# Expert rows of a top-1 mixture: indirect gathers with TensorE transposes replaced by 256-byte reads with a VectorE block transpose

## The chip, the cores and the metric

The kernel runs on one core of a Trainium2 chip. The metric is the device time in microseconds. Engines are named as in the profile: PE is TensorE (PEld its weight loads), DVE is VectorE, ACT is ScalarE, POOL is GpSimd and SP is SyncE, which here only issues DMAs. A name such as L345 is a line of the kernel.

## The reference

A linear attention with a normalised output feeds a mixture of eight experts in which each row goes to one expert.

```python
# q, k, v: (8 batches, 8 heads, 576 rows, 64), g_norm: (64,)
kv  = einsum('bhsd,bhse->bhde', k, v)
out = einsum('bhsd,bhde->bhse', q, kv)
out = out / sqrt(mean(out*out, -1) + 1e-6) * g_norm
x   = out.transpose(0, 2, 1, 3).reshape(4608, 512)      # N = 4608 rows, D = 512

logits = x @ w_gate                                     # (4608, 8)
e      = argmax(logits, 1)
gate   = softmax(logits)[n, e[n]]
y[n]   = gate[n] * (relu(x[n] @ w1[e[n]]) @ w2[e[n]])   # w1: (512, 1024), w2: (1024, 512) per expert
```

All inputs and the output are float32. With the inputs drawn here the experts get between 494 and 600 rows each.

## The kernel before

**Attention.** The loop runs over `b` from 0 to 8. In step `b` the PE work of batch `b` (the products of k and v, transposes of q, a product that folds the routing weights in) is interleaved with output tiles of 128 rows of the batches before it. Nine tiles make a pair of batches `j`; pair 3 ends in step `b == 8`. For a tile, `o_mm` does the products, `o_red` the squares (ACT) and their sums (DVE, `ms`), `o_nrm` the inverse root (ACT, `rs`), and `o_x` writes normalised float16 rows into a row buffer `xrow` of three tiles, of which there are four, and logits into `lhat`. The instructions are issued in the order of the program text; each engine works its own queue in order.

**Routing.** `route` takes a chunk of tiles (`chunks` lists them per pair), finds each row's expert and its place among that expert's rows by prefix sums on PE, and POOL scatters the rows (L743) into a DRAM table `x_slots`: 4608 slots of 516 two-byte words for each expert, 512 for the row and four for gate and row number. `route` is a generator, whose next part is run by `job()` twice per tile step.

**Experts.** A group is an expert and some of its slot tiles of 128. Of experts 0, 1 and 2 the first three tiles come first, as groups 0 to 2, with counts known after two thirds of the rows (`early_rows`); their last two tiles are groups 3 to 5; experts 3 to 7 have five tiles each, groups 6 to 10. One further tile for rows that don't fit (the spill tile, `d_` names) is put ahead of group 10, and a loop after the end takes what even that does not hold. With the inputs used here the spill tile is empty and the loop runs no time.

A group's rows come by `fetch`: POOL gathers 128 slots by an index (L291), where slots beyond the count have an index out of bounds and are skipped, so that the buffer, one of three `xl` set to zero at the start, keeps what it held. `xpose` turns a tile by four PE transposes (L325), and DVE evacuates it, times g_norm, into `xsT` (L328). `stage1` does the first product in eight steps of 128 columns (L345) with a Relu on ACT (L353); `stage2` does the second (L361), DVE multiplies by the gate (`y`, L366), and POOL scatters the result (L369). Both products have two PSUM buffers. The transposes of the next group stand between the `stage2` calls of the current one.

**Weights.** `w_step` casts one staged 512 KB piece to float16 on DVE (L220) and has SP load another (L206, L210). There are four staging buffers, and `w_step` is called at fixed places in the tile steps and the groups.

**End.** The last group's scatters are followed by `fin`, a small memset, and the loop, whose count each engine loads from memory. In the built order of POOL the last output scatter stands behind the loop's test.

Of the kernel before, what the change touches and what calls it, by code (L numbers as in the profile page):

```python
# [45 lines left out]
def kernel(  # L46
# [20 lines left out]
    xs_views = dram_disjoint_views(xs.ap(), NT)  # L67
# [9 lines left out]
    for j in range(4):  # L77
# [20 lines left out]
        "w1off": arf[:, None] + 128.0 * np.array([0, 2, 1, 3], np.float32)[None, :],  # L98
# [36 lines left out]
    nc.scalar.dma_start(g2[64:128, :], g_norm.unsqueeze(1))  # L135
    wgt = P_const.tile([128, 8, 8], F32, tag="wgt")
# [17 lines left out]
    chunks = {0: [(0, 9)], 1: [(0, 9)], 2: [(0, 3), (3, 9)], 3: [(0, 3), (3, 6), (6, 9)]}  # L154
    ohbs, n_route = [], 0
    for j in range(4):
# [7 lines left out]
    xl_ring = [  # L164
        P_const.tile([128, SLOT_TILES, ROW], I16, tag=f"xl{n}", name=f"xl{n}") for n in range(3)
    ]
# [13 lines left out]
    def w_load(pool, bufs):  # L180
# [23 lines left out]
        if n < 4:  # L204
            r0 = 128 * (2 * (n % 2) + n // 2)
            nc.sync.dma_start(st, w1[r0 : r0 + 128, :])  # L206
# [8 lines left out]
        w_staged.append((e, dst, st))  # L215

    def w_cast(engine):
        if w_staged:
            e, dst, st = w_staged.pop(0)
            engine.tensor_copy(dst, st)  # L220
            w_done[e] = w_done.get(e, 0) + 1
# [15 lines left out]
    cnt = P_const.tile([128, 8], F32, tag="cnt")  # L237
    srow = P_const.tile([128, 8, SLOT_TILES], F32, tag="srow")
# [4 lines left out]
    def row_index(name, ctr, ne, nk):  # L243
        bad = P_const.tile([128, ne, nk], F32, tag="bad" + name, name="bad" + name)
        nc.vector.tensor_tensor(
            bad, _bc(cv["srank"][:, 0:nk], 1, ne), _bc(ctr[:, 0:ne], 2, nk), op=ALU.is_ge
        )
        idx = P_const.tile([128, ne, nk], I32, tag="idx" + name, name="idx" + name)
        nc.vector.scalar_tensor_tensor(
            out=idx, in0=bad, scalar=BIG, in1=srow[:, 0:ne, 0:nk], op0=ALU.mult, op1=ALU.add  # L250
        )
        badi = P_const.tile([128, ne, nk], I32, tag="badi" + name, name="badi" + name)
        nc.vector.tensor_scalar(badi, bad, BIG, None, op0=ALU.mult)
        return idx, badi
# [3 lines left out]
    def early_rows():  # L258
# [6 lines left out]
        for i in range(EARLY):  # L265
            groups[i].fetch()
        yield

    def final_rows():
        nc.vector.tensor_tensor(cnt, base[n_route], cv["ebase"], op=ALU.subtract)  # L270
        rows["all"] = row_index("a", cnt, 8, SLOT_TILES)

    class Group:
        def __init__(self, n, e, k0, k1):
# [4 lines left out]
            self.xl = xl_ring[n % 3]  # L279
            self.table = "early" if self.small and k0 == 0 else "all"  # L280

# [6 lines left out]
        def fetch(self):  # L288
            idx = rows[self.table][0]
            for k in range(self.K):  # L290
                nc.gpsimd.indirect_dma_start(  # L291
                    out=self.xl[:, k, :], out_offset=None, in_=xs.ap(),
                    in_offset=IndirectOffsetOnAxis(
                        ap=idx[:, self.e, self.k0 + k : self.k0 + k + 1], axis=0
                    ),
                    bounds_check=E * N - 1, oob_is_err=False,
                )

        def slot_ids(self):
# [4 lines left out]
                self.xl[:, 0 : self.K, D + 2 : D + 4].bitcast(I32),  # L304
                badi[:, self.e, self.k0 : self.k0 + self.K].unsqueeze(2), op=ALU.max,
            )

# [6 lines left out]
        def start(self):  # L314
            self.xsT = self.pool().tile(
                [128, 4, self.n], F16, tag="xsT" + self.tag(), bufs=1, name="xsT"
            )

        def tag(self):
            return ""  # L320

        def xpose(self, k):
            ps = PSA.tile([128, 4, 128], F16, tag="KV", bufs=2, name="xps")
            for c in range(4):
                nc.tensor.transpose(  # L325
                    ps[:, c, :], self.xl[:, k, c * 128 : (c + 1) * 128].bitcast(F16), ident16
                )
            nc.vector.tensor_scalar(  # L328
# [49 lines left out]
    class SpillGroup(Group):  # L378
# [4 lines left out]
        def tag(self):  # L383
            return "d"
# [508 lines left out]
```

## Time and profile before

| what | us |
|---|---|
| median of three runs | 326.77 (325.64 to 333.92) |
| profiled execution | 330.94 |
| its span, from the first to the last instruction | 329.2 |
| PE busy | 269.0 (82%) |
| DVE busy | 183.4 (56%) |
| POOL busy | 137.6 (42%) |
| ACT busy | 119.9 (36%) |
| mean granted PE clock | 0.903 of full |

In a group's line, the numbers after the bar are the busy time in us and the mean of one instruction in ns; after the second bar stands how long the engine had been idle before these instructions, and what ended most of that. In the timeline a row has start, duration, engine, line, operation, output and inputs, and in brackets the idle time before it and what released it. A windows row has the stretch, its length, then busy time and count for PE, PEld, DVE, ACT and POOL, the granted PE clock, the share of the DMA engines and GB/s. In the slices a digit is the busy share in tenths.

### The profile page before, as it was taken

Reading aid. Unit: us, or ns where it says so; the run is one execution under the profiler, and the core shown is the slowest. Engines: PE = TensorE matmul, PEld = TensorE weight load, DVE = VectorE, ACT = ScalarE, POOL = GpSimd, SP = SyncE. Lnnn points to the kernel's source line nnn. Section 1 sums busy time; section 2 is a strip of 40 time slices with the busy share of each in tenths; the row PEclk is TensorE's granted clock in tenths of the full one; section 3 lists DMA queues with packets and bytes.
Section 4 is the critical chain, followed back from the end, with each engine's and each line's share of the span. In section 5 each row is a group of like instructions: output and inputs, shape, how many; then the busy total and the mean of one; then the engine's idle time right before and its main releaser. Section 6 shows DMA issues by size and latency. Waiting matters only on the chain.

```text
span 329.2 us, 7247 instructions
## 1 busy us (share of the span) xinstructions
PE 269.0 (82%) x2759; PEld 189.3 (58%) x2759; DVE 183.4 (56%) x433; ACT 119.9 (36%) x316; POOL 137.6 (42%) x147
## 2 busy tenths in 40 slices
PE   0699897689766977564979996989999999997980
PEld 0587776577656866462535563657565665645630
DVE  6205566346745368889184678344657658375040
ACT  1136564436543445322322431326142240602600
POOL 9100001720076004384675462777477656052041
PEclk9999997959995589555999998999999999999996
DMA  6999999997897016799589894667799999983021
GB/s 158 334 368 367 369 368 367 381 282 216 246 323 295 18 67 167 250 323 324 201 260 372 295 322 121 214 214 251 250 339 358 351 397 279 408 284 130 0 99 55
DMA packets 45395, 85.79 MB, mean 261 GB/s; under 512 B 6188, under 2 KB 22829, under 8 KB 45360
## 3 DMA queue, kind: packets, MB, share of 16 engines
q1 hardware_dynamic: 36736, 66.07, 59.9%
q0 software_dynamic: 6976, 18.96, 15.6%
q10 hardware_dynamic: 1648, 0.29, 0.5%
q8 instruction: 22, 0.36, 0.4%
q14 instruction: 13, 0.11, 0.1%
HBM read 71.77 MB, written 15.50 MB: 265 GB/s over the span
## 4 chain that ended last, share of the span: by engine, by line
PE 26%; issue 11%; DMA 9%; POOL 7%; DVE 5%; POOLq 1%; ACT 0%; DVEq 0%; ACTq 0%
PE hp L345 13%; PE yp L361 11%; DMA out_dram<-y,d_id 7%; POOL out_dram L369 4%; POOL xl L291 2%; DMA xl<-x_slots,idxe 2%; PE xps L325 1%; DVE y L366 1%; DMA x_slots<-xrow,posi 1%; POOL x_slots L743 1%; DVE w1e L220 1%; DVE xsT L328 0%; POOLq L888 0%; POOLq L854 0%; DVE w2e L220 0%
## 5 line engine op out<-in xcount | busy, mean ns | idle before, releaser
L353 ACT ACTIVATE hT<-hp 128x320 f16<-128x320 f32 (+3 forms) x136 | 53.6, 426 | 106.5 <-PE hp L345 105.9
L345 PE MATMUL hp<-xsT,w1e 128*128 128x320 f16 (+2 forms) x512 | 76.6, 306 | 7.2 <-DVE xsT L328 6.3
L361 PE MATMUL yp<-w2e,hT 128*128 128x512 f16 x320 | 74.1, 379 | 0.3 <-DVE y L366 0.3
L369 POOL DMA_INDIRECT out_dram<-y,idv x40 | 44.6, 1115 | 60.3 <-DVE y L366 49.3
L345 PEld LDWEIGHTS <-w1e 128*128 128x128 f16 x512 | 51.0, 100 | 32.1 <-issue 11.7
L651 PE MATMUL ops<-kvx,qT 64*128 64x72 f32 (+1 forms) x640 | 48.0, 310 | 10.5 <-DVE lhat L680 9.6
L743 POOL DMA_INDIRECT x_slots<-xrow,posi x36 | 35.7, 991 | 40.5 <-DVE xrow L739 15.5
L651 PEld LDWEIGHTS ops<-kvx,qT 64*128 64x128 f32 (+1 forms) x640 | 42.3, 215 | 15.0 <-issue 9.3
L361 PEld LDWEIGHTS <-hT 128*128 128x128 f16 x328 | 30.8, 98 | 31.6 <-issue 0.4
L366 DVE TENSOR_SCALAR y<-yp,xl 128x512 f32<-128x512 f32 x40 | 30.0, 750 | 33.6 <-PE yp L361 29.9
L664 DVE TENSOR_REDUCE ms<-sq 128x8 f32<-128x512 f32 x36 | 24.6, 685 | 25.1 <-ACT sq L660 25.0
L291 POOL DMA_INDIRECT xl<-x_slots,idxa x31 | 32.4, 1046 | 11.7 <-issue 7.0
L594 PE MATMUL kvps<-mk,mv 128*64 128x64 f32 x640 | 28.7, 258 | 9.4 <-DMA mv<-in_v_dram 9.1
L676 DVE TENSOR_TENSOR xrow<-ops,rs 128x512 f16<-128x512 f32 x36 | 24.7, 686 | 18.0 <-DMA x_slots<-xrow,posi 9.3
L660 ACT ACTIVATE sq<-ops 128x512 f32<-128x512 f32 x36 | 21.5, 598 | 31.9 <-PE ops L651 31.5
L594 PEld LDWEIGHTS kvps<-mk,mv 128*64 128x64 f32 x640 | 26.0, 168 | 11.8 <-issue 10.3
L710 POOL COPY xrow<-tokc 128x3 int32<-128x3 int32 x12 | 3.0, 253 | 64.3 <-DVE xrow L676 64.2
L582 PE MATMUL tps<-ctile,mq 128*128 128x128 f32 x144 | 26.9, 320 | 3.5 <-ACT qT L583 1.9
L220 DVE CAST w2e<-wst 128x1024 f16<-128x1024 f32 x32 | 22.3, 704 | 11.4 <-DMA wst<-in_moe_w_dram 11.4
L583 ACT COPY qT<-tps 128x384 f32<-128x384 f32 x48 | 21.9, 473 | 14.4 <-PE tps L582 14.4
L328 DVE TENSOR_SCALAR xsT<-xps,g 128x512 f16<-128x512 f16 x41 | 19.2, 477 | 12.9 <-PE xps L325 12.7
L220 DVE CAST w1e<-wst 128x1024 f16<-128x1024 f32 x32 | 21.6, 688 | 4.5 <-DMA wst<-in_moe_w_dram 4.5
(99 smaller groups left out, 184.1 us busy)
## 6 DMA issues: line engine op xcount, KB each, us to landing
wst<-in_moe_w_dram SPq DMA_DIRECT2D x64, 512.0 KB, 5.8
mq<-in_q_dram SPq DMA_DIRECT2D x16, 576.0 KB, 7.8
mk<-in_k_dram SPq DMA_DIRECT2D x16, 320.0 KB, 7.5
mv<-in_v_dram SPq DMA_DIRECT2D x16, 320.0 KB, 7.3
mk<-in_k_dram SPq DMA_DIRECT2D x16, 256.0 KB, 7.9
mv<-in_v_dram SPq DMA_DIRECT2D x16, 256.0 KB, 7.1
wsts<-in_moe_w_dram SPq DMA_DIRECT2D x8, 512.0 KB, 5.9
out_dram<-y,idv POOLq DMA_INDIRECT x40, 4.9
```

The costliest lines, as they stand in the source:

```text
L220: engine.tensor_copy(dst, st)
L291: nc.gpsimd.indirect_dma_start(out=self.xl[:, k, :], out_offset=None, in_=xs.ap(), in_offset=IndirectOffsetOnAxis(ap=idx[:, self.e, self.k ...
L345: nc.tensor.matmul(hp, self.w()[0][:, kk, f * 128 : (f + 1) * 128], self.xsT[:, kk, s : s + self.step], start=(kk == 0), stop=(kk == 3),)
L353: nc.scalar.activation(self.hT[:, f, s : s + self.step], hp, ACTF.Relu)
L361: nc.tensor.matmul(yp, self.hT[:, f, k * 128 : (k + 1) * 128], self.w()[1][:, f, :], start=(f == 0), stop=(f == 7),)
L366: nc.vector.tensor_scalar(y, yp, self.xl[:, k, D : D + 2].bitcast(F32), None, op0=ALU.mult)
L369: nc.gpsimd.indirect_dma_start(out=self.views(k), out_offset=IndirectOffsetOnAxis(ap=self.ids[:, k : k + 1], axis=0), in_=y, in_offset=Non ...
L582: nc.tensor.transpose(ps[:, c, :], src[:, 128 * m : 128 * m + 128], cv["ident"])
L594: nc.tensor.matmul(kvps[b][64 * y : 64 * y + 64, 2 * u + a, :], main["v", b, u][:, 2 * y + a, c, :], main["k", b, u][:, 2 * y + a, c, :], ...
L651: nc.tensor.matmul(ps[p0 : p0 + 64 * n, y, o0 : o0 + 72], qT[b][hs, a, blk // 2 : blk // 2 + n, :].rearrange("d c p -> d (c p)"), kvx[b][h ...
L676: nc.vector.tensor_tensor(xr[:, 0:D].bitcast(F16).rearrange("p (a h d) -> p a h d", a=2, h=4), xv, _bc(rs2, 3, 64), op=ALU.mult,)
L743: nc.gpsimd.indirect_dma_start(out=xs_views[9 * j + t0 + t], out_offset=IndirectOffsetOnAxis(ap=posi[:, t : t + 1], axis=0), in_=xrow[j, ( ...
```

## The change

- The gathers go. `fetch` reads a group's rows, which lie together in `x_slots`, with four plain DMAs into 32 partitions each, in pieces of 128 words (256 B), and the gate and row number with a fifth. They are issued from ACT's queue, but for groups 0 and 1, which SP issues in step `b == 8`.
- Slots beyond the count must then hold zeros in DRAM. `pads` has POOL scatter a row of zeros to them once counts are known; the index of a used slot is out of bounds, so it is skipped. Three groups' `pads` follow the early counts, two groups' the final ones, and the others are issued two or three groups ahead.
- The PE transposes and the `xsT` evacuations go. `xpose` is one DVE instruction for the group that transposes 32x32 blocks, issued after the second `y` of the group before. `stage1` reads the blocks in place. For that the rows of w1 go to PE in another order, and g_norm is applied as a scale in the w1 cast (`g4`). The spill tile keeps PE transposes.
- Also: six `xrow` buffers, not four; the folded product uses the other PSUM pair and both its copies are on ACT; small groups' second product uses that pair too; pair 2 is routed as tiles 0 to 5 and 6 to 8; one more pause in `route`; one `w_step` per tile from step 5 on; in step 8 groups' work begins from its second tile; the zeroing of `xl` and `fin` go; the loop's count is loaded earlier, inside group 7.

```diff
-    chunks = {0: [(0, 9)], 1: [(0, 9)], 2: [(0, 3), (3, 9)], 3: [(0, 3), (3, 6), (6, 9)]}
+    chunks = {0: [(0, 9)], 1: [(0, 9)], 2: [(0, 6), (6, 9)], 3: [(0, 3), (3, 6), (6, 9)]}
...
-            r0 = 128 * (2 * (n % 2) + n // 2)
-            nc.sync.dma_start(st, w1[r0 : r0 + 128, :])
+            nc.sync.dma_start(st, w1.rearrange("(p c) f -> c p f", c=4)[n])
...
+            if n < 4:
+                engine.tensor_scalar(dst, st, g4[:, n : n + 1], None, op0=ALU.mult)
+            else:
+                engine.tensor_copy(dst, st)
...
-        for i in range(EARLY):
-            groups[i].fetch()
+        groups[0].pads()
+        yield
+        groups[1].pads()
+        groups[2].pads()
...
         rows["all"] = row_index("a", cnt, 8, SLOT_TILES)
+        for n in range(EARLY, EARLY + 2):
+            groups[n].pads()
...
-        def fetch(self):
-            idx = rows[self.table][0]
+        def pads(self):
+            pad = rows[self.table][0]
             for k in range(self.K):
                 nc.gpsimd.indirect_dma_start(
-                    out=self.xl[:, k, :], out_offset=None, in_=xs.ap(),
-                    in_offset=IndirectOffsetOnAxis(
-                        ap=idx[:, self.e, self.k0 + k : self.k0 + k + 1], axis=0
+                    out=self.pad_views[k],
+                    out_offset=IndirectOffsetOnAxis(
+                        ap=pad[:, self.e, self.k0 + k : self.k0 + k + 1], axis=0
                     ),
+                    in_=zrow, in_offset=None,
                     bounds_check=E * N - 1, oob_is_err=False,
                 )
+        def fetch(self, engine=nc.scalar):
+            r0 = self.e * N + 128 * self.k0
+            src = xs.ap()[r0 : r0 + self.n].rearrange("(g b) w -> b g w", b=32)
+            self.xl = self.pool().tile([128, self.n // 32, 128], I16, tag="xl", bufs=2, name="xl")
+            for i in range(4):
+                c0 = 128 * (2 * (i % 2) + i // 2)
+                engine.dma_start(self.xl[32 * i : 32 * i + 32], src[:, :, c0 : c0 + 128])
+            self.gi = P_fe.tile([128, SLOT_TILES, 4], I16, tag="gi", bufs=3, name="gi")
+            engine.dma_start(
+                self.gi[:, 0 : self.K],
+                xs.ap()[r0 : r0 + self.n, D:ROW].rearrange("(k p) w -> p k w", p=128),
+            )
+        def xpose(self):
+            g = self.n // 32
+            self.xT = self.pool().tile([128, g, 4, 32], I16, tag="xT", bufs=2, name="xT")
+            nc.vector.transpose(self.xT, self.xl.rearrange("p g (a c) -> p g c a", c=4))
...
-                if f == 0 and 1 <= real and EARLY <= real + 2 < len(groups):
-                    groups[real + 2].fetch()
+                if f == 0 and EARLY - 1 <= real < len(groups) - 3:
+                    groups[real + 3].pads()
...
                 cur.stage2(k)
                 if not cur.small:
                     w_step()
-                while todo and len(todo) > max(cur.K - 2 - k, 0):
-                    nxt.xpose(todo.pop(0))
+                if k == 0 and 0 <= real < len(groups) - 2:
+                    groups[real + 2].fetch()
+                if k == min(1, cur.K - 1) and 0 <= real < len(groups) - 1:
+                    groups[real + 1].xpose()
+                if k == 3 and cur.e == E - 2:
+                    spill.xpose()
...
-            nc.vector.tensor_copy(kvx[b][:, 1], folds[b][1])
+            nc.scalar.copy(kvx[b][:, 1], folds[b][1])
...
-                    [128, 3, ROW], I16, tag="xrow", bufs=4, name=f"xrow{j}{t}"
+                    [128, 3, ROW], I16, tag="xrow", bufs=6, name=f"xrow{j}{t}"
...
-                for _ in range((0, 1, 1, 2)[max(b - 5, 0)]):
+                if b >= 5:
                     w_step()
-                if b == B and n >= 3:
+                if b == B and n == 0:
+                    for i in range(2):
+                        groups[i].fetch(nc.sync)
+                if b == B and n >= 1:
                     unit()
                     unit()
...
-    fin = P_const.tile([128, 1], F32, tag="fin")
-    nc.gpsimd.memset(fin, 0.0)
-    manual.close()
...
-    with tc.For_i(0, n_more) as it:
+    with tc.For_i(0, n_more[0]) as it:
```

## The prediction

> **What bounds the kernel now.** I read, in this order, the page's slices, the windows by stage, the chain that ended last, the timeline where the chain breaks, and the groups by form; a fence for each.
>
> ```profile
> PE   0699897689766977564979996989999999997980
> DVE  6205566346745368889184678344657658375040
> PEclk9999997959995589555999998999999999999996
> DMA  6999999997897016799589894667799999983021
> ```
>
> ```profile
> 153.10:191.65 38.55, 35.60 (x205) 18.69 (x205) 21.08 (x51) 11.90 (x25) 22.14 (x23) 0.96 0.84 293
> 191.65:222.07 30.42, 26.15 (x182) 16.87 (x180) 19.00 (x53) 9.20 (x24) 18.49 (x19) 0.94 0.63 206
> 240.68:259.12 18.44, 18.44 (x126) 11.29 (x125) 11.89 (x24) 6.12 (x16) 13.30 (x13) 1.00 0.97 352
> 320.03:329.20 9.17, 0.00 (x1) 0.00 (x0) 0.75 (x1) 0.00 (x0) 1.60 (x3) 0.67 0.18 68
> ```
>
> A slice is 8.23 us. Up to about 66 us the DMA row is full (input loads). From 66 to 153 us nothing is full. From 153 us, where the expert stage starts, PE sets the time: a five-tile expert takes 18.4 us with PE busy throughout, DVE busy 11.9 and DMA at 0.97. The end, 9.2 us, has no matmul.
>
> ```profile
> 234.82 0.22 PE xps L325 x4
> 235.05 1.73 PE yp L361 x8
> ...
> 240.68 8.69 PE hp L345 x64
> ```
>
> ```profile
> 100.33 0.69 DVE L676 TENSOR_TENSOR xrow<-ops,rs 128x512 f16<-128x512 f32 x1 [5.01 <-DMA x_slots<-xrow,posi]
> 101.26 1.98 PE L651 MATMUL ops<-kvx,qT 64*128 64x72 f32 x16 [3.21 <-DVE lhat L680]
> 153.12 2.72 PE L345 MATMUL hp<-xsT,w1e 128*128 128x384 f16 x8 [2.78 <-DVE xsT L328]
> 202.96 5.54 PE L345 MATMUL hp<-xsT,w1e 128*128 128x256 f16 x32 [3.12 <-DVE xsT L328]
> ...
> 301.16 0.98 POOL L369 DMA_INDIRECT out_dram<-y,d_id  x1 [3.81 <-DVE y L366]
> 325.20 0.98 POOL L369 DMA_INDIRECT out_dram<-y,idv  x1 [4.67 <-issue]
> ```
>
> ```profile
> L328 DVE TENSOR_SCALAR xsT<-xps,g 128x512 f16<-128x512 f16 x41 | 19.2, 477 | 12.9 <-PE xps L325 12.7
> L291 POOL DMA_INDIRECT xl<-x_slots,idxa x31 | 32.4, 1046 | 11.7 <-issue 7.0 <-DMA x_slots<-xrow,posi 2.6 <-PE hp L345 2.1
> ```
>
> In the chain, a tile's transposes cost PE 0.22 us, its second matmuls 1.73, a five-tile first stage 8.69. At 100.33 DVE had stood 5.01 us because row buffers (four) still had scatters in flight, and PE then ran at half clock to about 118. At 202.96 PE waited behind the spill tables on DVE. The last output scatter started at 325.20, 4.4 us after its data (DVE done at 320.82), because the built order puts the loop test ahead of it.
>
> [...] 32 matmuls of 256 columns take 5.54 us after the 3.12 us wait and 4.30 elsewhere. [...]
>
> **Part 1, removed from PE.** 40 x 4 transposes: 40 x 0.22 = 8.8 us on PE's path; the empty spill tile keeps its four. With them go 40 xsT evacuations (19.2 us of DVE).
>
> **Part 2, the block transpose on DVE.** One instruction per group, 512 elements per tile. [...] 1.76 us for three tiles, 1.22 for two, 2.82 for five: 22 us in all, so DVE's sum hardly moves. Its place matters. In the built order it stands behind the second y of the current group. For five tiles: yp of tile 1 ends at 3.46 us of the second stage, y at 4.35, a cast at 4.9, the transpose at 7.7, y of tile 2 at 8.4. yp has two PSUM buffers, so tile 4, due at 6.92, waits until 8.4: 1.5 us lost, against 1.1 us of transposes gained. For two tiles it stands after the last y: the next group starts 4.35 + 1.22 = 5.6 us into a 3.46 us stage, 2.1 us late; ahead of a five-tile group, 3.7 late. For three tiles, 0.85 late. Bounds: a quarter of this price [...] to the full price[...].
>
> **Part 3, casts and small edits.** 32 of the expert casts, and four of the spill's, get a per-partition scale; [...] 0.69 us stays (up to twice that, 0.4 us each more, if not: 14 us of DVE, partly hidden under PE). Eight kvx copies move to ACT (0.39 each), which has room. Eight g4 loads and 8 casts earlier by one stage: hidden under the loads.
>
> **Part 4, early gain.** Six row buffers remove the 5.01 us wait. Five tile steps took 22.9 us from 95.58 to 118.45; at the pace of the warm stretch (seven in 23.2 us from 72.4) they take 16.5. Gain 6.4, so the fifth tile of the last two batches starts near 127, not 133.1.
>
> **Part 5, start of the expert stage.** Counts at about 122 us; POOL: three row scatters, then nine zeroing scatters. The scatter of the spill tile at 301.16 writes nothing (the reference's inputs give 494 to 600 rows per expert, below 640) and still took 0.98 us, so skipping is not cheap: 9 x (0.98 + 0.30) = 11.5 us, from 123.3 to 135, landed near 138 (2.6 us is the shortest landing of such scatters). SP, which waits there, issues 4 reads at 0.65 us (a small-piece load on ACT's queue took 0.67), landing near 143; transpose 1.8; first matmul near 144.9, against 153.1: gain 8.2, the 6.4 included. Weight loads queued behind SP wait with them, one or two of them late, covered by the four staging buffers.
>
> **Part 6, first three groups.** Now three attention tiles and two routing rounds stand between these matmuls. From 144.9: f0 and f1 at half clock 2.7 us; PE then stands 2.9 us for the last routing; at 164 the second half of group 0; block-transpose delays 0.85 + 0.85 + 0.5. ACT's read for group 2 waits for the row scatters of the sixth to third last tiles (landed 165.5), and five issues of 0.65 us hold its Relus until 169: PE 1.6 us late. The read for group 3 waits for the last rows and four zeroing scatters (180.5): 2.3 us more. Group 3 starts near 194.2, 49.3 us after the first matmul; before took 38.5. Loss 10.8.
>
> **Part 7, the two-tile groups.** POOL per group: two outputs and five zeroing scatters, 2 x 1.48 + 5 x 1.28 = 9.4 us, for 7.8 us of matmuls. The read on ACT waits for the newest zeroing scatters, though its own landed long ago, and the first Relus of the next group stand behind it: about +2.2 and +0.6. With the transposes (+1.3 behind the spill tables, +2.05, +1.9), 38.4 us against 30.4. Loss 8.
>
> **Part 8, five-tile groups and end.** Three groups at 17.34 + 1.5 = 18.84 against 18.5: +1.0. In the one before the spill tile, y of tile 2 (8.4) is followed on DVE by a cast, y, a cast and the spill's three copies, so PE starts its last tile near 11.5 instead of 6.92 and ends 21.9 us after the group began, against 17.4: +4.5. The 3.1 us wait at 299.6, for the last group's xsT, goes. Together +2.4. The end gains 3.7, because the last scatter no longer stands behind the loop test: 320.03 + 9.2 becomes the last matmul + 5.5 (y 0.75, issue 1.3, landing 3).
>
> Sum: -8.2 + 10.8 + 8 + 2.4 - 3.7 = +9.3, span 329.2 -> 338.5. The profiled execution took 330.94 around that span; its median of runs is 326.77, ratio 0.987. (338.5 + 1.7) x 0.987 = 336.
>
> **Rivals.** (a) *Cheap block transpose at a quarter of my price* (0.8 us for five tiles). Saved: start 1.2, small groups 2.2, two-tile groups 3.6, five-tile groups 6, and about 2.5 of half-clock time: 15.5, so 323 span, 319 us: faster. For: the data are 2-byte, and 2-byte xsT took 477 ns where 512 single elements from PSUM took 750. [...] It decides below about 0.85 us for five tiles. (b) *Half price* (1.4 us), or the front gaining as much again from the freed PSUM ring: 11 less, 326 us: no change. (c) *DMA becomes the bound.* 20,480 pieces of 256 B and 5,120 of 8 B replace 5,120 rows; DMA stands at 0.97 at 352 GB/s and the fullest windows show 1.07 at 368. If a piece costs 40 ns of an engine, a five-tile group needs 15 us for weights and outputs and 7 for rows, 22 against 18.8: about +12 over the stage, 348 us. [...]
>
> **How the numbers follow.** Forecast 0.50, at 336, own range 328 to 344, of which 0.07 lies within 2%; (c) 0.18; (b) 0.14; (a) 0.18. Slower 0.43 + 0.18 = 0.61, same 0.21, faster 0.18; two per cent is what a measurement of this kernel can tell from no change. The range 314 to 351 takes in most of (a) and (c); outputs and waits that stack in small groups set its upper end.
>
> **What would show it.** Right: no xrow wait near 95 us; first expert matmul near 145; transposes of about 1.8, 1.2 and 2.8 us with PE waiting behind them for y; Relus late behind reads on ACT between 165 and 225; the last scatter within 1 us of its y. Wrong: a five-tile transpose near 1 us or five-tile groups of 17.5 us (a, b); casts waiting for wst in most groups and DMA above 1.0 after 230 us (c); zeroing scatters well under 0.98 us, or ACT never waiting.

## The result and the profile after

The changed kernel takes 371.51 us (median of four runs, 368.7 to 377.48), the kernel before 328.54 (four runs, 325.64 to 333.92): ratio 1.1313, 95% interval 1.1134 to 1.1492. The forecast was slower, 336 us with a range of 314 to 351: the direction is right, the size is not. Of the four executions of each kernel the slowest (377.48 and 333.92) counts as slow, and the ratio is taken over the other three. The profiled execution took 368.7 us, its span 366.9; it is the shortest of the four, and the profiled one of before (330.94) lies above its median, so the stages below account for 37.7 us where the medians are 43.0 apart.

A correction first. The texts above say that the experts get 494 to 600 rows and that the spill tile is empty. Counted again from the reference's inputs, the experts get 564, 494, 600, 572, 539, 654, 585 and 600: expert 5 has 14 rows more than its five tiles hold, so the spill tile holds 14 rows, and the scatter at 301.16 in the trace of before wrote 14 rows, not none. That a scatter which writes nothing takes as long, 0.98 us, is shown by others, the changed kernel's zeroing scatters (last section).

The slices of the page, now 9.17 us each:

```profile
PE   0699999986595226996777176619889498987990
DVE  0106686773688436677178030700855617476030
PEclk9999999999579558699899586757999969998996
DMA  5999999999977376888883518190696799996012
```

Up to about 80 us PE is fuller than before. Then come holes that before did not have: at 120 to 140 us PE falls to 2 tenths, and between 200 and 250 us twice to 1 tenth, with the granted clock at 5 tenths. Windows for the same stages as those shown of before (groups 0 to 2, groups 3 to 5, one five-tile group, the end):

```profile
135.64:187.68 52.04, 42.19 (x224) 21.31 (x224) 31.55 (x73) 14.78 (x35) 23.17 (x25) 0.87 0.81 257
187.68:235.35 47.67, 26.72 (x145) 16.19 (x145) 21.00 (x49) 8.89 (x24) 19.90 (x21) 0.77 0.46 120
266.39:287.20 20.81, 17.80 (x105) 10.16 (x104) 12.93 (x21) 6.02 (x16) 8.37 (x8) 1.00 0.80 277
358.22:366.90 8.68, 0.00 (x0) 0.00 (x0) 0.75 (x1) 0.00 (x0) 1.48 (x2) 0.64 0.21 75
```

In the second row PE is busy 26.72 of 47.67 us (before 26.15 of 30.42), and DMA stands at 0.46: on average neither an engine nor DMA is full, so something waits. The timeline of the group after them, the first five-tile one (group 6), shows who waits for whom:

```profile
232.46 2.83 DVE L327 STREAM_TRANSPOSE xT<-xl 128x2560 int16<-128x2560 int16 x1
...
234.85 1.20 POOL L302 DMA_INDIRECT x_slots<-zrow,pada  x1 [0.30 <-issue]
...
235.35 4.43 PE L363 MATMUL hp<-xT,w1e 128*128 128x320 f16 x16 [3.59 <-DVE xT L327]
...
235.96 1.03 SPq L211 DMA_DIRECT2D wst<-in_moe_w_dram  x2
...
237.22 24.36 SPq L207 DMA_DIRECT2D wst<-in_moe_w_dram  x4
237.31 5.86 ACTq L317 DMA_DIRECT2D xl<-x_slots  x4
...
237.75 1.06 POOL L387 DMA_INDIRECT out_dram<-y,idv  x1 [0.30 <-issue]
...
246.90 0.38 ACTq L319 DMA_DIRECT2D gi<-x_slots  x1
247.33 1.43 ACT L371 ACTIVATE hT<-hp 128x320 f16<-128x320 f32 x4 [18.60 <-DMA xl<-x_slots]
248.14 8.24 PE L363 MATMUL hp<-xT,w1e 128*128 128x320 f16 x48 [8.37 <-ACT hT L371]
...
249.78 0.98 POOL L302 DMA_INDIRECT x_slots<-zrow,pada  x1 [10.96 <-DMA gi<-x_slots]
...
257.71 3.38 ACTq L317 DMA_DIRECT2D xl<-x_slots  x4
```

Read it from PE backwards. PE fills its two PSUM buffers from 235.35, stands from 239.78 on, and goes on 8.37 us later, when a Relu has emptied one. ACT works in order and has reads of `x_slots` ahead of that Relu. They wait for zeroing scatters, the last of which POOL issued at 234.85, and start at 237.31. Up to there ACT has waited and PE has not. What PE then waits for is the reads themselves: the four take 5.86 us to issue, where four at 188.21 take 1.84, and `gi` follows only at 246.90: in the trace its issue waits for the semaphore on which the first of the four counted its landing and on which `gi` then counts its own, and that read landed just before, 9.5 us after its own issue. Four weight loads of 512 KB are in flight with them (two at 235.96 and the first two of the row at 237.22; its other two are issued after 259), and from 238 to 248 us the DMA engines are full: 0.51 of their time goes to weight loads and 0.44 to the reads. So the scatters push the reads out of PE's second stage, in which ACT has nothing to do, into the place where the Relus and the weight loads are.

On POOL the next zeroing scatter (249.78) has waited 10.96 us, until those reads had landed, since it writes the table that they read; only when POOL is through with the scatters can the next reads go (257.71). The two queues hold each other up. They do so by the table as a whole: the reads at 237.31 fetch the rows of group 7, and the scatters that they wait for zero slots of group 8, other rows. Whether a table for each expert would untie them was not tried. And PE, after such waits, does 48 matmuls of 320 columns in 8.24 us, where 64 take 8.86 at a granted clock of 1.00 (340.73 to 349.59).

The waits over the whole execution (total us, times, longest):

```profile
ACT hT L371 <- DMA xl<-x_slots: 63.8, 5, 18.6
...
POOL x_slots L302 <- DMA gi<-x_slots: 41.2, 5, 11.0
PE hp L363 <- ACT hT L371: 34.2, 8, 8.4
...
PE hp L363 <- DVE xT L327: 23.3, 7, 14.0
```

Of the 34.2 us that PE stands behind Relus, 2.7 belong to an attention tile (145.94). In the seven other places PE comes to a stand before the first read has started only in group 2 (171.46, reads from 172.63) and group 4 (201.33, reads from 206.48), 6.3 us together. In the other 25 the scatters have landed, and ACT is issuing the reads that they held back. In group 7 it is again `gi` that comes late (268.42), here behind a weight load that SP issued at 261.26, on whose semaphore it waits and which landed just before, 7.1 us after its issue.

The balance by stage is in the first two rows of the table below: the expert stage starts 17.5 us earlier, groups 0 to 5 take 30.7 longer, groups 6 to 10 with the spill tile 24.9 longer, the end 0.5 less; but for rounding the sum is the 37.7 us of more span.

Of the runs below, beside e5 to e16 the kernel before itself took 353 to 361 us. The traces kept there show a longer attention stage (e13, the changed kernel again, has its first expert matmul at 160.6 us, not 135.6), for a reason that they don't show, so that between these and the others only ratios to the kernel before on the same chip, and stages after the first expert matmul, are compared.

### The profile page after: what moved, and what is told of

Read it like the earlier page. It is cut to its first block, busy times and chain, and to the rows that moved or that the text cites. A ratio compares the mean times of both kernels' runs of the same rounds, so it can differ in the third digit from the quotient of the medians.

```text
span 366.9 us, 6972 instructions
## 1 busy us (share of the span) xinstructions
PE 263.1 (72%) x2599; PEld 174.6 (48%) x2599; DVE 181.9 (50%) x398; ACT 119.5 (33%) x324; POOL 128.0 (35%) x144
## 3 DMA queue, kind: packets, MB, share of 16 engines
q10 hardware_dynamic: 24384, 4.79, 8.0%
## 5 line engine op out<-in xcount | busy, mean ns | idle before, releaser
L363 PE MATMUL hp<-xT,w1e 128*128 128x320 f16 (+2 forms) x512 | 90.0, 339 | 58.2 <-ACT hT L371 34.2
L363 PEld LDWEIGHTS <-w1e 128*128 128x128 f16 x512 | 55.2, 109 | 92.0 <-issue 59.9
L384 DVE TENSOR_SCALAR y<-yp,gi 128x512 f32<-128x512 f32 x40 | 29.7, 741 | 85.5 <-PE yp L379 85.5
L302 POOL DMA_INDIRECT x_slots<-zrow,pada x31 | 31.9, 1030 | 58.5 <-DMA gi<-x_slots 41.2
L699 PE MATMUL ops<-kvx,qT 64*128 64x72 f32 (+1 forms) x640 | 42.9, 285 | 11.1 <-DVE lhat L728 10.3
L699 PEld LDWEIGHTS ops<-kvx,qT 64*128 64x128 f32 (+1 forms) x640 | 37.4, 191 | 17.0 <-DVE lhat L728 8.2
L642 PE MATMUL kvps<-mk,mv 128*64 128x64 f32 x640 | 25.8, 242 | 11.9 <-DMA g<-in_g_norm_dram 8.4
L222 DVE TENSOR_SCALAR w1e<-wst,g 128x1024 f16<-128x1024 f32 x32 | 24.5, 775 | 13.9 <-DMA wst<-in_moe_w_dram 13.9
L642 PEld LDWEIGHTS kvps<-mk,mv 128*64 128x64 f32 x640 | 23.2, 154 | 14.4 <-issue 10.7
L327 DVE STREAM_TRANSPOSE xT<-xl 128x2560 int16<-128x2560 int16 (+2 forms) x11 | 23.2, 2109 | 9.0 <-DMA xl<-x_slots 9.0
L708 ACT ACTIVATE sq<-ops 128x512 f32<-128x512 f32 x36 | 21.6, 601 | 13.4 <-PE ops L699 12.5
```

The costliest lines, as they stand in the source:

```text
L302: nc.gpsimd.indirect_dma_start(out=self.pad_views[k], out_offset=IndirectOffsetOnAxis(ap=pad[:, self.e, self.k0 + k : self.k0 + k + 1], axis=0
L363: nc.tensor.matmul(hp.rearrange("p (g b) -> p g b", b=32), self.w()[0][:, kk, f * 128 : (f + 1) * 128], self.xcols(kk, s), start=(kk == 0) ...
L384: nc.vector.tensor_scalar(y, yp, self.gate(k), None, op0=ALU.mult)
L642: nc.tensor.matmul(kvps[b][64 * y : 64 * y + 64, 2 * u + a, :], main["v", b, u][:, 2 * y + a, c, :], main["k", b, u][:, 2 * y + a, c, :], ...
L699: nc.tensor.matmul(ps[p0 : p0 + 64 * n, y, o0 : o0 + 72], qT[b][hs, a, blk // 2 : blk // 2 + n, :].rearrange("d c p -> d (c p)"), kvx[b][h ...
```

## The experiments

The theory (A): the reads on ACT's queue wait for zeroing scatters in front of the Relus, and the scatters on POOL wait for the reads. Rival B: the reads wait for completion semaphores (slots, in the expectations) that SP's weight loads hold. Rival C: the block transposes and their place on DVE are the loss.

Stages in us, from each trace; the last column has the time (a single execution, or the median where the text gives an interval) and that of the kernel before on the same chip:

| kernel | first expert matmul | groups 0 to 5 | groups 6 to 10 | after the last matmul | time, kernel before beside it |
|---|---|---|---|---|---|
| before | 153.1 | 69.0 | 98.0 | 9.2 | 328.5 |
| changed | 135.6 | 99.7 | 122.9 | 8.7 | 371.5, 328.5 |
| e1 reads on SP | 134.0 | 86.3 | 112.0 | 8.7 | 342.8, 325.4 |
| e2 zeroing after the read | 134.0 | 90.0 | 126.0 | 8.5 | 360.2, 325.4 |
| e3 zeroed once, ACT | 149.8 | 84.1 | 107.2 | 14.8 | 357.8, 325.4 |
| e4 zeroed once, SP | 155.0 | 83.4 | 104.8 | 14.8 | 359.8, 325.4 |
| e5 SP, units later | 163.2 | 86.6 | 110.2 | 9.1 | 370.8, 358.1 |
| e6 and transposes early | 166.2 | 83.5 | 111.9 | 8.8 | 372.2, 358.1 |
| e7 and early tiles by writes | 162.1 | 83.7 | 113.1 | 18.4 | 379.0, 358.1 |
| e8 changed, four xrow | 161.4 | 101.7 | 115.7 | 9.0 | 389.6, 358.1 |
| e9 = e6 | 163.1 | 81.7 | 112.4 | 8.5 | 367.4, 360.6 |
| e10 zeroed on POOL, SP, later, early | 171.9 | 68.5 | 103.2 | 8.4 | 353.8, 360.6 |
| e11 e10, transposes late | 172.7 | 75.6 | 105.6 | 8.4 | 364.1, 360.6 |
| e12 e10, units early | 170.4 | 76.1 | 103.2 | 8.4 | 359.9, 360.6 |
| e13 changed again | 160.6 | 98.6 | 120.6 | 8.2 | 388.7, 353.4 |
| e14 changed, four xrow | 157.9 | 99.0 | 119.5 | 8.9 | 388.8, 353.4 |
| e15 before, front edits | 156.2 | 68.9 | 100.0 | 10.0 | 340.7, 353.4 |
| e17 = e1 | 139.0 | 87.5 | 110.9 | 8.9 | 346.2, 326.8 |
| e18 before, fold ring | 147.5 | 68.1 | 98.5 | 10.5 | 326.9, 326.8 |

**The queue of the reads (e1, e17).**

```diff
-        def fetch(self, engine=nc.scalar):
+        def fetch(self, engine=nc.sync):
```

> All slot reads are issued by SP instead of ACT; the zeroing scatters stay where they are. In the changed kernel PE stood 34.2 us behind Relus (8 times), and the Relus behind reads that waited on ACT. Theory A (the reads on ACT wait for zeroing scatters, and these for earlier reads, in front of the Relus): PE's wait for Relus falls below 8 us, POOL's zeroing scatters still wait for reads (over 20 us of the 41.2), SP's weight loads now stand behind the waiting reads; span 366.9 -> 335 to 345. Rival B (completion slots that the reads share with SP's weight loads are what ACT waits for): the same place is freed, and in SP's own order a slot wait costs nothing new; span near 330 to 340, so A and B are not told apart here. Rival C (the block transposes and their place on DVE cost the time): PE's waits move from Relus to xT, span stays above 358.

> The kernel of e1 (changed kernel with all slot reads on SP's queue), timed. Theory (reads in front of the Relus on ACT are the largest part of the loss): ratio to the kernel before 1.03 to 1.07, where the changed kernel has 1.10 to 1.13. Rival (e1 was a lucky look): ratio 1.09 to 1.13.

Span 341.0 in e1; e17 timed gives ratio 1.0606, interval 1.0528 to 1.0684, against 1.1313. Waits in e1:

```profile
POOL x_slots L302 <- DMA gi<-x_slots: 28.2, 6, 6.0
PE hp L363 <- DVE xT L327: 26.9, 6, 13.6
...
DVE w1e L222 <- DMA wst<-in_moe_w_dram: 21.8, 7, 7.0
...
PE hp L363 <- ACT hT L371: 3.6, 2, 2.7
```

PE's wait behind Relus is 3.6 us instead of 34.2. The scatters still wait for the reads, 28.2 us, and the weight loads, now behind the reads on SP, come late (21.8), but PE has no wait for a cast of them that the trace lists. One word takes back 13.4 us in groups 0 to 5 and 10.9 in groups 6 to 10: 24.3 of the 55.6 that the expert stage had lost. PE's wait for the block transposes stays (26.9, was 23.3), so what came back is not C's; how much C costs is measured with e11 below. A and B aren't told apart by this.

**The zeroing (e2, e3, e4).** e2 moves `pads` behind `fetch`:

```diff
-                if f == 0 and EARLY - 1 <= real < len(groups) - 3:
-                    groups[real + 3].pads()
...
                     groups[real + 2].fetch()
+                    if EARLY - 1 <= real < len(groups) - 3:
+                        groups[real + 3].pads()
```

e3 and e4 zero each expert's five slot tiles once, at `b == 1`, on ACT's queue, and leave `pads` without scatters; e4 has the reads on SP.

```diff
+    def zero_all():
+        for e in range(E):
+            nc.scalar.dma_start(
+                xs.ap()[e * N : e * N + SLOTS].rearrange("(p s) w -> p s w", s=SLOT_TILES),
+                _bc(zrow, 1, SLOT_TILES),
+            )
```

> The zeroing scatters for the group three ahead are issued after the reads for the group two ahead instead of before them, so a read waits only for zeroing scatters a whole group older; reads stay on ACT. Theory A: ACT's wait in front of Relus falls from about 45 us to under 15, PE's wait behind Relus from 34.2 to under 12; zeroing scatters still wait for the reads just issued, with output scatters behind them on POOL; span 340 to 350. Rival B (completion slots): the wait at the read of gi behind SP's weight loads stays, PE behind Relus over 20 us, span above 355. Rival C (transposes): over 358, with PE waiting for xT.

> No zeroing scatters at all: the five slot tiles of each expert are zeroed once by eight plain writes (5.3 MB) from ACT's queue at the start of the second batch; reads stay on ACT. Theory A: neither side of the mutual wait is left; PE behind Relus under 8 us; from the first expert matmul to the last one 222.6 us falls to about 178, and the start, which stood 11.6 us behind nine zeroing scatters, comes from 135.6 to 124, plus up to 15 us for the extra writes in the stretch where DMA is full; span 311 to 326. Rival B: reads on ACT still wait for completion slots of SP's weight loads; PE behind Relus stays over 15 us, the expert stage over 195 us, span above 330. Rival C: the expert stage stays over 210 us, span above 345.

> As the run before, with all reads on SP. Theory A: nothing was left to wait for on ACT but the short issues (2.3 us a group), so the expert stage is within 5 us of the run before, either side, since the weight loads now carry the issues. Rival B: the reads on ACT were held by slots, so SP is better by more than 10 us. Rival C: no difference between the two, both slow (over 345).

e2 missed what A expected: its span is 358.4 us and PE stands 20.0 us behind Relus, near what B expected (above 355, over 20). Groups 0 to 5 gain 9.7 us, groups 6 to 10 lose 3.1. The scatters wait 47.6 us for reads and so run late, and the next reads wait for them just the same: a whole group's distance in the program is none in time when the two queues are tied. Two waits of e2's ACT, and the place of the second in the timeline:

```profile
ACT hT L371 <- DMA xl<-x_slots: 34.2, 3, 18.5
...
ACT hT L371 <- DMA wst<-in_moe_w_dram: 11.8, 1, 11.8
```

```profile
257.02 0.38 ACTq L319 DMA_DIRECT2D gi<-x_slots  x1
257.51 1.43 ACT L371 ACTIVATE hT<-hp 128x320 f16<-128x320 f32 x4 [11.78 <-DMA wst<-in_moe_w_dram]
```

Here a weight load, not a scatter, ends the wait of `gi` on ACT (the fourth read was issued by 250.2): B exists. Against B as the main cause stands e3, which leaves the reads on ACT and takes only the scatters away: 31.3 of the 55.6 us come back, PE stands 6.3 us behind Relus (A expected under 8, B over 15), and from the first expert matmul to the last are 191.4 us (A about 178, B over 195). B's price where no scatter is left is e3 against e4, which differ in the queue alone: 0.7 us in groups 0 to 5 and 2.4 in groups 6 to 10, about as much as the same kernel's stages differ from one execution to another (e1 and e17 by 1.1, the changed kernel and e13 by 1.1 and 2.3). So A carries most. In the changed kernel itself the two act together, since the scatters push the reads among the weight loads, and there these runs don't separate them. What e4 leaves, against e1, is the price of the zeroing with the reads on SP: 2.9 and 7.2 us. In all, taking the reads off ACT and the zeroing out gives back 34.4 of the 55.6 us that the expert stage had lost.

The spans of e3 and e4 are over the estimate because the writes held ACT: at 40.23 us a square had waited 16.40 us behind them, and the expert stage starts 14 to 19 us later. In e3, e4 and e7, which have such writes on ACT, the time after the last matmul is longer: 14.8, 14.8 and 18.4 us, in the changed kernel 8.7. Why is open.

**The order of the units and the place of the transposes (e5, e6, e7, e9, e10, e11, e12).** All have the reads on SP. e5 begins the expert units two tiles later; e6 and e9 also issue `xpose` ahead of `stage2` and the spill tile's in the first stage; e7 also zeroes the first three groups' tiles by three plain writes on ACT's queue at the start, and `early_rows` calls no `pads`.

```diff
-                if b == B and n >= 1:
+                if b == B and n >= 3:
...
+            if 0 <= real < len(groups) - 1:
+                groups[real + 1].xpose()
             for k in range(cur.K):
                 cur.stage2(k)
...
-                if k == min(1, cur.K - 1) and 0 <= real < len(groups) - 1:
-                    groups[real + 1].xpose()
-                if k == 3 and cur.e == E - 2:
-                    spill.xpose()
```

> Reads on SP as in the first experiment (span 341.0), and the expert units begin two attention tiles later in the built order (n >= 3, as in the kernel before, instead of n >= 1). Theory: PE is in order, and in the changed kernel the first expert matmul stands in front of three attention tiles while it waits 13.7 us for its transpose; with the tiles put ahead of it, they fill that wait, the last counts are known 12 to 20 us earlier, and the first three groups run undivided. First matmul stays at 134 to 137, group 3 starts 8 to 12 us earlier than 183.2; span 329 to 333. Rival: the stretch is bound by DVE's routing and the row scatters on POOL, so that the order on PE moves nothing: group 3 within 3 us of 183, span 338 to 344.

> The run before, and each block transpose issued ahead of the current group's second stage (DVE is idle there) instead of behind its second y; the spill tile's transposes go into the first stage of the group ahead of it. Theory: the place of the transposes on DVE costs PE what the trace of e1 shows: 1.4 us behind y in each of three five-tile groups, 4.0, 2.0 and 5.8 us ahead of the groups that follow two-tile groups, 0.8 twice, about 6 at the spill tile, 24 in all, with clock; span falls by 16 to 24 against e5, to about 310. Rival: the reads, on SP behind waits for zeroing scatters, come just in time, and the earlier transpose only waits for them on DVE, with casts behind it: gain under 8 us.

> The run before, and the nine zeroing scatters of the first three groups are left out; three plain writes at the start of the kernel (1.2 MB) zero these slot tiles instead. Theory: the nine scatters (11.6 us on POOL) hold the first read: first expert matmul 134 -> 124 to 130 (attention tiles now fill part of the wait), span 4 to 10 us below e6. Rival: the row scatters and the last counts set the time, so the start moves but group 3 doesn't: under 3 us.

> The kernel of e6 once more, beside a run of the kernel before of 325 us if the front isn't held up as it was there (PE stood 6 us at 64 us waiting for nothing that the trace showed). Theory: the place of the transposes and of the units is worth 24 us against e1: ratio to the kernel before about 0.98, span near 317. Rival (reads just in time, DVE then stands in front of the transposes): ratio 1.02 to 1.05, DVE waiting over 10 us for xl.

e5 does not shorten groups 0 to 5 (86.6, e1 86.3), but 5.71 us of it is a stall at 197 us for nothing that the trace shows, so it leaves open what the order of the units is worth. e6 and e9 miss: the rival is right. In e9:

```profile
DVE xT L327 <- DMA xl<-x_slots: 22.8, 4, 9.2
```

The transpose stands earlier, but its rows have not come: the reads wait for the zeroing. DVE waits, with casts and `y` behind it, and groups 6 to 10 take 112.4 us as in e1. e7 has its first expert matmul 4 us before e6 and its last 2.7 before; it takes longer only by the time after its last matmul (18.4 us, e6 8.8). Its writes delay the first loads (PE stood 8.47 us at 22.83).

So the same three edits were tried without zeroing scatters: e10 has `zero_all` on POOL's queue at the start; e11 puts the transposes back, e12 the units.

> No zeroing scatters (the slot tiles zeroed once, now by eight plain writes on POOL's queue at the start, where POOL is idle), reads on SP, units two tiles later, transposes ahead of the second stage. Theory: with neither the mutual wait nor the transposes in the way, the expert stage needs its matmuls: from the first expert matmul to the last 160 to 170 us (before 166.9, changed kernel 222.6), start at 125 to 135, span 295 to 312. Rival: the 5.3 MB of zeroes delay the loads of the front by their 15 us, start 140 to 150, span 312 to 325. Second rival: weight loads on SP, mixed with reads, come late and hold the expert stage above 180 us.

> As e10, but the transposes at their place in the changed kernel, behind the second y. Theory (prediction, parts 2 and 7): that place costs 1.4 us in each of three five-tile groups, 3.6 ahead of the first, 2.0 and about 4 at the two-tile groups, 0.8 twice and 4.2 at the spill tile: 19 us more than e10 in the expert stage. Rival: DVE's place matters little because the weight loads set the pace: under 8 us.

> As e10, but with the expert units where the changed kernel has them (n >= 1). Theory: PE waits for the first transpose with three attention tiles behind it: 6 to 14 us more than e10 at the start of group 3. Rival: without zeroing scatters the first read comes so early that PE hardly waits: within 3 us.

> The kernel of e10 (slot tiles zeroed once by plain writes on POOL's queue, no zeroing scatters, reads on SP, units two tiles later, transposes ahead of the second stage), timed. Theory: expert stage 160 to 172 us, so 45 to 60 below e13, of which the zero writes in the front give back 15 to 25; ratio to the kernel before 0.94 to 1.00, to e13 about 0.85. Rival (weights late on SP): expert stage over 180, ratio to the kernel before above 1.02.

From the first expert matmul to the last e10 takes 171.7 us (expected 160 to 170), the changed kernel 222.6, before 166.9. The place of the transposes (e11) costs 9.5 us, half of the 19 expected; that of the units (e12) 7.6; together they are about what e10 is better than e4 (16.5). With the 34.4 of the reads and the zeroing this makes 50.9 of the 55.6 us. The windows of e10, groups 3 to 5 and 6 to 10:

```profile
212.90:240.40 27.50, 23.83 (x146) 14.69 (x145) 20.38 (x47) 9.20 (x24) 6.79 (x7) 0.94 0.87 227
240.40:343.61 103.21, 94.98 (x565) 54.71 (x563) 56.89 (x81) 32.63 (x88) 31.64 (x29) 0.97 0.76 254
```

Groups 3 to 5 are now 2.9 us shorter than before (30.42). Group 6 takes 17.3 us against 18.4: the 1.1 us fit the five times 0.22 of PE transposes of part 1. In groups 7 and 8 (18.7 and 22.0 us) casts wait for weights, whose loads stand behind reads on SP (`w2e` 10.4 us in all), and the gain is gone. The expert stage is 22.4 us shorter than in e9, but the first matmul comes at 171.9, 8.8 us after e9's (5.7 after that of e6, the same kernel), so the writes give part of that back. Timed (e16): 354.24 against 353.39, ratio 1.0040, interval 1.0005 to 1.0074, so no better than the kernel before.

**The front (e8, e13 to e15, e18).** e8 and e14 have four `xrow` buffers (`bufs=4` instead of 6) in the changed kernel, e13 is the changed kernel; e15 is the kernel before with the other edits of the front, e18 with the first of them alone:

```diff
-                PSA.tile([128, 4, 72], F32, tag="T", bufs=2, name=f"fold{b}{y}")
+                PSA.tile([128, 4, 72], F32, tag="KV", bufs=2, name=f"fold{b}{y}")
...
-            nc.vector.tensor_copy(kvx[b][:, 1], folds[b][1])
+            nc.scalar.copy(kvx[b][:, 1], folds[b][1])
...
             yield
+            yield
             ex = rt("ex", [128, T, 8])
...
-    chunks = {0: [(0, 9)], 1: [(0, 9)], 2: [(0, 3), (3, 9)], 3: [(0, 3), (3, 6), (6, 9)]}
+    chunks = {0: [(0, 9)], 1: [(0, 9)], 2: [(0, 6), (6, 9)], 3: [(0, 3), (3, 6), (6, 9)]}
```

> The changed kernel with four xrow buffers instead of six. The prediction gave the two buffers the whole gain of the front, 6.4 us; measured was 16.7 us at the fifth tile of the last two batches (133.1 -> 116.4). If the buffers are the cause, the 5 us wait of xrow for its scatters and the half clock after it come back, and that tile starts at 125 to 133. If the other edits of the front (the fold's PSUM ring, kvx copies on ACT, the extra stage in the routing) are, it starts at 116 to 121. Span 367 plus what the front loses.

> The changed kernel as it is, as the reference on this chip for the three runs beside it: ratio to the kernel before 1.11 to 1.15, PE behind Relus 25 to 40 us.

> The changed kernel with four xrow buffers instead of six (the kernel of e8). Theory (buffers): DVE's waits of xrow for its row scatters come back (9 us in the kernel before), the fifth tile of the last two batches starts 8 to 14 us later than in e13; time 2 to 4% above e13. Rival (the other edits of the front): under 1% above e13, that tile within 3 us.

> The kernel before with the fold in the KV ring, both kvx copies on ACT, the extra stage in the routing and the cut of the third pair's routing at tile 6 as in the changed kernel; xrow stays at four buffers, nothing else of the change. Theory (buffers): ratio 0.99 to 1.01, DVE still waits about 9 us for xrow. Rival (these edits): ratio 0.96 to 0.98.

> The kernel before with one edit of the front: the fold's PSUM tiles come from the ring of the q transposes and k-v products (KV) instead of the ring of the routing (T). Theory: the ring is what frees PE and DVE in the front, and the result lies with e15, ratio 0.96 to 0.985. Rival: the kvx copies on ACT or the routing's extra stage bring it, ratio 0.99 to 1.01 here.

e8, a single execution, starts the expert stage at 161.4 us, e13 at 160.6 and e14 at 157.9; PE behind Relus is 26.9 us in e13, as expected, but its ratio to the kernel before, 1.0994 (1.0847 to 1.1142), is below the 1.11 to 1.15 expected. e14's ratio, 1.1061 (1.0943 to 1.1178), overlaps it, and in e14 DVE waits 1.3 us in all for row scatters: the two buffers show no effect here. On this chip the front is slower for another reason, though, so what they are worth where the first matmul came at 135.6 us is not shown. Four of the other edits do show an effect: e15 has ratio 0.9717, interval 0.9593 to 0.9842, and with four buffers its `xrow` never waits for a scatter. Its expert stage, 168.9 us, is not shorter than that of before in its trace (166.9), so the gain should lie in the front. It beats both kernels. It was run only on that chip. The fold's ring alone (e18, 1.0041, 1.0003 to 1.0079) brings nothing, and the two waits of `xrow` are still there:

```profile
DVE xrow L676 <- DMA x_slots<-xrow,posi: 9.0, 2, 5.1
```

Which of the others brings it, the copies on ACT, the extra stage, the cut or two of them together, was not tried and stays open. e18 also starts the expert stage at 147.5 us with a median equal to that of before: so some 5 us of the 17.5 by which the changed kernel starts earlier may be spread of executions.

## Why the prediction was wrong in size

- **Parts 1 and 2, transposes.** Right. Predicted, as the author's estimate (before has no such instruction), 1.76, 1.22 and 2.82 us; measured, by form:

```profile
L327 DVE STREAM_TRANSPOSE xT<-xl 128x2560 int16<-128x2560 int16 x5 | 14.2, 2836 | 0.0
...
L327 DVE STREAM_TRANSPOSE xT<-xl 128x1536 int16<-128x1536 int16 x3 | 5.3, 1771 | 9.0 <-DMA xl<-x_slots 9.0
...
L327 DVE STREAM_TRANSPOSE xT<-xl 128x1024 int16<-128x1024 int16 x3 | 3.7, 1234 | 0.0
```

  From the longest and the shortest of them this is 1.04 ns for an element of a partition plus 0.17 us. The wait for `y` behind the five-tile one was predicted at 1.5 and is 1.37 (at 264.67), that ahead of the first five-tile group 3.7 and is 3.59. Rival (a) and the half price of (b) fall. The other half of (b), a front that gains as much again, came true in size (part 4), but not by the freed PSUM ring (e18).
- **Part 3.** Nearly: casts with a scale take 775 ns on average (32 of them), 0.09 us more than the 0.69 kept (the `w1e` casts without a scale took 688 ns before).
- **Part 4, early gain.** Mis-sized: the gain is 16.7 us at the fifth tile of the last pair (116.36), not 6.4. The step took one wait of `xrow` for the cause; before has two (9.3 us in all), and e15 gains by four other edits of the front without more buffers. How the 16.7 us split between the two is open, since e14 and e15 ran where the front is slower.
- **Part 5, start.** The nine zeroing scatters are right: 116.56 to 128.2. The first matmul is at 135.64, not 144.9: 6.7 us because the scatters start at 116.56 and not at 123.3 (part 4), the rest because the reads were cheaper: 0.47 us each to issue, not 0.65, and the transpose starts 4.3 us after the first issue.
- **Part 6 and 7, small groups.** Predicted 18.8 us lost, measured 30.7. The mechanism, reads on ACT behind the newest zeroing scatters, was named; its size was 1.6, 2.3, 2.2 and 0.6 us, and the waits of PE for Relus in groups 2 to 5 are 5.10, 2.42, 8.00 and 2.87. The step counted POOL's work (9.4 us a group) but not that the zeroing scatters themselves wait for the reads, up to 10.96 us a time, with the output scatters in line behind them.
- **Part 8, five-tile groups.** This step failed: predicted +2.4, measured +24.9. It has no term for reads that wait for zeroing scatters: by POOL's work there is room (five outputs and five zeroing scatters, 13.8 us, in a group of 18.8), and the prediction looks for late Relus between 165 and 225 us only. The mutual wait goes on in these groups, because it is a chain of landings and not of work: PE stood 8.37, 1.00 and 3.83 us for Relus in groups 6, 7 and 8. With the reads on SP 10.9 of the 24.9 go, without zeroing 7.2 more, and e10 ends at +5.2.
- **The end.** Predicted 3.7 us gained, measured 0.5. The last scatter does start at once (359.29, its `y` is done at 359.0) and lands 3.3 us later, no later than predicted (4.3 with its issue). What has no term is the rest: after the landing the engines need another 4.3 us to finish, where in before 1.3 us were left, because they had gone through the loop's end ahead of the scatter. (The terms given, 0.75, 1.3 and 3, add up to 5.05 and not to 5.5.)
- **Rival (c), DMA.** Refuted: the reads' queue has 24,384 packets in 8.0% of 16 engines, 19 ns each by 0.080 x 16 x 366.9 us / 24,384, not the 40 that it needed. DMA stands at 0.80 in a five-tile group. The pieces are not free, though: between 238 and 248 us, where the engines are full, they took 26 ns each.
- The start was 9.3 us better than predicted, the small groups 11.9, the five-tile groups 22.5 and the end 3.2 worse: with rounding the 28.4 us between 338.5 and 366.9. It is luck that the total is not further off: the start hides 9.3 of the 34.4 us by which the expert stage was missed.

## What to carry to other kernels

A DMA that must wait should not be issued by an engine whose next instructions are on the critical path (moving the reads from ACT to SP gave back 24.3 us here): price its wait to the landing of the last writer, not its issue, and ask beside which other transfers it will then run. When one queue writes a table that another reads, follow both directions, since here a read that waits for a write and a write that waits for the earlier read made a chain in which the landings counted and not the work: ACT stood 63.8 us in front of Relus behind such reads and POOL 41.2 for their landing, while DMA was at 0.46 in groups 3 to 5, and with a whole group's distance between the two in the program POOL still stood 47.6 (e2). Edits that ride along deserve an experiment of their own: here four of them were the only part with which a kernel was faster.

## What the runs showed of the hardware

- An indirect scatter with every index out of bounds wasn't cheap: the zeroing scatters of a five-tile group's first three tiles skip all 128 slots here, and the first of them took POOL 0.98 us (249.78 above), where the scatters of rows take 0.99 on average.
- A DMA on one queue waited for the landing of a load on another: `gi` on ACT for an SP weight load, 6.8 us after the read before it (e2, 250.2 to 257.02).
- The packets of ACT's queue, 17,408 of 24,384 of them pieces of 256 B (34 tiles x 512), took 19 ns of a DMA engine each on average over the changed kernel, and 26 ns from 238 to 248 us, where the engines were full.
- Behind an 8.4 us wait PE was also slower: the granted clock was 0.50 from 238 to 250 us and 0.80 over the 48 matmuls behind the wait, which took 8.24 us, against 6.6 by the pace of 64 in 8.86.
